# Reading a two-byte scalar by a 16-partition broadcast instead of a single-partition load, in a streaming multiply-add

## The chip, the cores and the metric

One core of a Trainium2 chip. The metric is device time in microseconds (us) of one execution; the median of several executions is quoted. The kernel before takes 152.79 us (3 runs, 152.72 to 152.88). The profile's own span, from the first to the last instruction, is about 1.8 us shorter (150.6 us).

## The reference

```python
B, S, D = 512, 32, 640            # x, fx: bf16; alpha: one bf16 number
def reference(x, fx, alpha):
    return x + alpha * fx
```

x, fx and the result are 20.97 MB each: 62.9 MB have to be moved for one multiply and one add per element.

## The kernel before

The tensors are seen as 128 partitions of 81,920 elements and cut into five chunks of 16,384 columns (4 MB each, 32 KB per partition). All bulk transfers go through SyncE's queue; alpha alone goes through ScalarE's. TensorE multiplies a row of ones by alpha, which puts alpha on all 128 partitions, and VectorE copies it out of PSUM.

```python
def alpha_to_lanes(nc, consts, psum, alpha, eng):     # eng = nc.scalar
    P = nc.NUM_PARTITIONS
    a_1 = consts.tile([1, 1], alpha.dtype, name="a_1")
    eng.dma_start(out=a_1[:], in_=alpha[None, :])
    ones = consts.tile([1, P], alpha.dtype, name="ones")
    nc.vector.memset(ones[:], 1.0)
    a_ps = psum.tile([P, 1], F32, name="a_ps")
    nc.tensor.matmul(a_ps[:], ones[:], a_1[:], start=True, stop=True)
    a_f = consts.tile([P, 1], F32, name="a_f")
    nc.vector.tensor_copy(out=a_f[:], in_=a_ps[:])
    return a_f

# ... cut: views, pools (four buffers for x, two for fx), load_x, load_f, store ...
    a_f = alpha_to_lanes(nc, consts, psum, alpha, nc.scalar)

    def compute(k, parts=1):                # x_t = f_t * a_f + x_t, on VectorE
        n = CHUNK // parts
        for j in range(parts):
            s = bass.ts(j, n)
            nc.vector.scalar_tensor_tensor(
                out=xt[k][:, s], in0=ft[k][:, s], scalar=a_f[:],
                in1=xt[k][:, s], op0=ALU.mult, op1=ALU.add)

    load_x(0); load_f(0); load_x(1); load_f(1); load_x(2)
    compute(0)                              # first reader of a_f
    load_f(2); store(0); load_x(3)
    compute(1)
    # ... cut: the same pattern to chunk 4, whose store is cut in two
```

## Time and profile before

| what | value | where it is read |
|---|---|---|
| time | 152.79 us | the timed runs |
| DMA engines | 418 GB/s, 9 tenths busy or more nearly throughout | the slices of the page |
| VectorE | 86.9 us busy, 49.5 us waiting for fx | the page, the view of waits |
| alpha landed | 1.87 us | the trace's semaphore records |
| first multiply-add starts | 22.84 us | the timeline |

First the page of the kernel before: its span, the busy tenths of the DMA engines and the GB/s in 40 slices of 3.8 us, and the packets. q1 is SyncE's queue, q10 is ScalarE's.

```profile
span 150.6 us, 85 instructions
DMA  6999999999999999799999999999999999999994
GB/s 200 444 453 435 418 418 418 418 444 453 444 453 435 418 418 418 339 444 470 418 418 418 418 418 435 435 435 453 426 435 444 418 418 435 435 435 405 426 444 205
DMA packets 2306, 62.92 MB, mean 418 GB/s; under 512 B 258, under 2 KB 258, under 8 KB 258
q10 hardware_dynamic: 2, 0.00, 0.0%
```

There is no slice in which the DMA engines rest: the kernel is a stream of transfers. The packets can be counted: 2048 rows of data and 256 semaphore packets (the 4-byte write with which an engine reports its share of a transfer as moved; 16 bulk transfers of 16 each) on q1, and on q10 one 2-byte data packet and one 4-byte semaphore packet, alpha's.

The start of the timeline of the kernel before. Columns: start in us, duration in us, engine (ACTq and SPq are the issuing queues), line, operation, and in brackets how long the engine had been idle and what released it.

```profile
0.73 0.38 SPq L59 DMA_DIRECT2D x_t<-in_x_dram  x1
0.73 0.49 ACTq L20 DMA_DIRECT2D a<-in_alpha_dram  x1
1.92 0.16 PE L24 MATMUL a_ps<-a,ones 1*128 1x1 bf16 x1 [1.92 <-DMA a<-in_alpha_dram]
2.11 0.16 DVE L26 COPY a_f<-a_ps 128x1 f32<-128x1 f32 x1 [1.13 <-PE a_ps L24]
22.84 17.28 DVE L69 SCALAR_TENSOR_TENSOR x_t<-f_t,a_f,x_t 128x16384 bf16<-128x16384 bf16 x1 [20.57 <-DMA f_t<-in_fx_dram]
```

a_f is ready at 2.27 us, and its first reader starts at 22.84 us, released by the load of f_t. Alpha has 20.6 us of slack to its first use.

The view of waits of the kernel before (engine, line, what it waited for: us in all, times, longest):

```profile
DVE x_t L69 <- DMA f_t<-in_fx_dram: 49.5, 5, 20.6
PE a_ps L24 <- DMA a<-in_alpha_dram: 1.9, 1, 1.9
```

Two lines of its chain of waits (start, duration, what):

```profile
40.16 21.99 DMA f_t<-in_fx_dram
79.55 41.16 DMA f_t<-in_fx_dram
```

### The profile page before, as it was taken

Reading aid. Unit: us, or ns where it says so; the run is one execution under the profiler, and the core shown is the slowest. Engines: PE = TensorE matmul, PEld = TensorE weight load, DVE = VectorE, ACT = ScalarE, POOL = GpSimd, SP = SyncE. Lnnn points to the kernel's source line nnn. Section 1 sums busy time; section 2 is a strip of 40 time slices with the busy share of each in tenths; the row PEclk is TensorE's granted clock in tenths of the full one; section 3 lists DMA queues with packets and bytes.
Section 4 is the critical chain, followed back from the end, with each engine's and each line's share of the span. In section 5 each row is a group of like instructions: output and inputs, shape, how many; then the busy total and the mean of one; then the engine's idle time right before and its main releaser. Section 6 shows DMA issues by size and latency. Waiting matters only on the chain.

```text
span 150.6 us, 85 instructions
## 1 busy us (share of the span) xinstructions
PE 0.2 (0%) x1; PEld 0.1 (0%) x1; DVE 86.9 (58%) x8; POOL 0.2 (0%) x4
## 2 busy tenths in 40 slices
PE   0000000000000000000000000000000000000000
PEld 0000000000000000000000000000000000000000
DVE  0000009999679998499991006999900089997000
POOL 0000000000000000000000000000000000000000
DMA  6999999999999999799999999999999999999994
GB/s 200 444 453 435 418 418 418 418 444 453 444 453 435 418 418 418 339 444 470 418 418 418 418 418 435 435 435 453 426 435 444 418 418 435 435 435 405 426 444 205
DMA packets 2306, 62.92 MB, mean 418 GB/s; under 512 B 258, under 2 KB 258, under 8 KB 258
## 3 DMA queue, kind: packets, MB, share of 16 engines
q1 hardware_dynamic: 2304, 62.92, 98.0%
q10 hardware_dynamic: 2, 0.00, 0.0%
HBM read 41.94 MB, written 20.97 MB: 418 GB/s over the span
## 4 chain that ended last, share of the span: by engine, by line
DMA 56%; DVE 29%; DVEq 6%; issue 0%; SPq 0%
DMA f_t<-in_fx_dram 56%; DVE x_t L69 29%; DVEq L131 6%; SPq L59 0%; DVEq L69 0%
## 5 line engine op out<-in xcount | busy, mean ns | idle before, releaser
L69 DVE SCALAR_TENSOR_TENSOR x_t<-f_t,a_f,x_t 128x16384 bf16<-128x16384 bf16 (+1 forms) x6 | 86.6, 14439 | 49.5 <-DMA f_t<-in_fx_dram 49.5
L26 DVE COPY a_f<-a_ps 128x1 f32<-128x1 f32 x1 | 0.2, 159 | 1.1 <-PE a_ps L24 1.1
L22 DVE MEMSET ones<- 1x128 bf16 x1 | 0.2, 165 | 0.8 <-PEq L120 0.8
L24 PE MATMUL a_ps<-a,ones 1*128 1x1 bf16 x1 | 0.2, 159 | 1.9 <-DMA a<-in_alpha_dram 1.9
L120 POOL MEMSET const-bfloat16-1.0<- 128x1 bf16 x1 | 0.1, 102 | 0.0
L120 POOL MEMSET const-uint8-127<- 128x1 uint8 x1 | 0.1, 102 | 0.0
L24 PEld LDWEIGHTS <-ones 1*128 1x128 bf16 x1 | 0.1, 100 | 1.0 <-DVE ones L22 1.0
L120 POOL MEMSET const-float32-0.0<- 128x1 f32 x1 | 0.1, 99 | 0.2 <-issue 0.2
L120 POOL MEMSET const-float32-1.0<- 128x1 f32 x1 | 0.1, 99 | 0.0
## 6 DMA issues: line engine op xcount, KB each, us to landing
x_t<-in_x_dram SPq DMA_DIRECT2D x5, 4096.0 KB, 34.8
f_t<-in_fx_dram SPq DMA_DIRECT2D x5, 4096.0 KB, 32.1
out_dram<-x_t SPq DMA_DIRECT2D x4, 4096.0 KB, 36.5
out_dram<-x_t SPq DMA_DIRECT2D x2, 2048.0 KB, 15.2
a<-in_alpha_dram ACTq DMA_DIRECT2D x1, 0.0 KB
```

Source lines behind the costliest of these rows:

```text
L22: nc.vector.memset(ones[:], 1.0)
L24: nc.tensor.matmul(a_ps[:], ones[:], a_1[:], start=True, stop=True)
L26: nc.vector.tensor_copy(out=a_f[:], in_=a_ps[:])
L69: nc.vector.scalar_tensor_tensor(out=xt[k][:, s], in0=ft[k][:, s], scalar=a_f[:], in1=xt[k][:, s], op0=ALU.mult, op1=ALU.add,)
L120: nc = _bacc.Bacc("TRN2", target_bir_lowering=False, num_devices=1)
L131: with _tile.TileContext(nc) as tc:
```

## The change

Alpha is loaded to 16 partitions by one broadcast transfer, so that each of the 16 DMA engines makes one 2-byte read; the matmul still takes only the first row. The likely intent is to spread the little transfer over the engines rather than to leave it on one.

```diff
-    a_1 = consts.tile([1, 1], alpha.dtype, name="a_1")
-    eng.dma_start(out=a_1[:], in_=alpha[None, :])
+    a_1 = consts.tile([16, 1], alpha.dtype, name="a_1")
+    eng.dma_start(out=a_1[:], in_=alpha.to_broadcast((16, 1)))
     ones = consts.tile([1, P], alpha.dtype, name="ones")
     nc.vector.memset(ones[:], 1.0)
     a_ps = psum.tile([P, 1], F32, name="a_ps")
-    nc.tensor.matmul(a_ps[:], ones[:], a_1[:], start=True, stop=True)
+    nc.tensor.matmul(a_ps[:], ones[:], a_1[0:1, :], start=True, stop=True)
```

## The prediction

> **What bounds the kernel now.** The DMA engines. The slices row of the page shows them at 9 tenths nearly throughout, 418 GB/s over the span of 150.6 us. The trace's packet records add up: 1792 rows of 32 KB at 1.213 us (median) and 256 of 16 KB at 0.611 us make 112 x 1.213 + 16 x 0.611 = 145.6 us on each of 16 engines. The first bulk packet starts at 1.74 us and the last store lands at 149.76 us, 148.0 us in all, so only about 2.4 us of an engine's stretch is not steady streaming. VectorE is busy 86.9 us (58%) and waits 49.5 us for the fx loads (the view of waits). The chain of waits is 56% DMA of f_t.
>
> **Where alpha stands.** The timeline: its transfer is issued at 0.73 us on ScalarE's queue (0.49 us of issue), the matmul starts at 1.92 us, the copy to a_f is over at 2.27 us. The first multiply-add waits for f_t until 22.84 us. Alpha's chain has 20.6 us of slack. It now moves two packets (2 bytes of data, 7 ns; 4 bytes of semaphore, 9 ns), at 1.58 us, just ahead of the first bulk packet.
>
> **What the change does.** It adds 15 data and 15 semaphore packets, one pair on each engine: an estimate from the two records is 16 ns of busy time an engine. The Trainium skill ("DMA: Bandwidth & Descriptors", section "Why a DMA increments its semaphore by 16 and not by 1") says that a [1,1] scalar uses one engine and that the slowest dimension of both sides sets the number, so 16 here. This trace agrees for before: one data packet, and two updates of alpha's semaphore (1.30 us, 1.87 us). Bytes moved, the order of the bulk transfers, the matmul (1x1), the copy and VectorE's work stay as they are.
>
> **Worth.** (a) Alpha's chain: if its packets queue behind the first bulk packets (1.6 to 2.4 us long), it lands at about 3.5 to 4.5 us instead of 1.87 us; still 18 us of slack, so nothing. (b) Busy time: 0.02 us an engine. (c) What can reach the end is a later start of the bulk stream, since the stream is the bound: 16 engines' descriptors of alpha are made at the same time as those of the first x load. The issues in the timeline take 0.33 to 0.57 us; a delay of 0 to 0.3 us of the first load is my estimate from those. (d) Evening out one 16 ns pair over the engines gains nothing.
>
> **Prediction.** 152.9 us, 8 times in 10 within 152.3 to 153.6 us. Faster by over 2%: 1%; within 2%: 98%; slower by over 2%: 1%.
>
> **What shows each step.** Alpha's queue: 32 packets instead of 2; packets under 512 B 288 instead of 258. Idle time of TensorE before the matmul: 1.9 us now, between 1.9 and 4.5 us after. Start of the first multiply-add: 22.8 us, later by no more than 0.3 us, ended by DMA f_t and not by a_f. Gap between 418 GB/s and after's mean: under 0.3%. VectorE busy time: 86.9 us unchanged. First bulk packet: 1.7 to 2.0 us.
>
> **What would make it wrong.** Alpha landing after 22 us, because its packets starve behind the bulk queue on some engine (then the first multiply-add would name the matmul's copy); a lasting phase shift between engines that slows the loads and stores together; or the tiny reads of one address stalling an engine for several us rather than for 16 ns.

## The result, and the profile after

The changed kernel takes 152.84 us (4 runs, 152.58 to 152.95), the kernel before on the same occasions 152.75 us (4 runs, 152.33 to 152.88). The ratio is 1.0008 with a 95% interval of 0.9985 to 1.0031: the same. (A ratio here is the mean time of one kernel's fast runs over the mean of the other's fast runs of the same rounds, so it is not quite the ratio of the medians quoted.)

The page of the changed kernel:

```profile
span 151.0 us, 85 instructions
DMA  6999999999999999899999999999999999998994
GB/s 208 443 434 434 425 417 417 434 443 451 443 434 434 417 417 399 347 460 434 425 434 417 417 417 425 451 469 434 417 443 417 417 425 425 460 469 360 425 443 187
DMA packets 2336, 62.92 MB, mean 417 GB/s; under 512 B 288, under 2 KB 288, under 8 KB 288
q10 hardware_dynamic: 32, 0.00, 0.0%
```

30 more tiny packets, as expected, and the same stream. Now the start of its timeline:

```profile
0.73 0.57 ACTq L20 DMA_DIRECT2D a<-in_alpha_dram  x1
0.73 0.38 SPq L59 DMA_DIRECT2D x_t<-in_x_dram  x1
8.19 0.16 PE L24 MATMUL a_ps<-a,ones 1*128 1x1 bf16 x1 [8.19 <-DMA a<-in_alpha_dram]
8.38 0.16 DVE L26 COPY a_f<-a_ps 128x1 f32<-128x1 f32 x1 [7.41 <-PE a_ps L24]
22.84 17.29 DVE L69 SCALAR_TENSOR_TENSOR x_t<-f_t,a_f,x_t 128x16384 bf16<-128x16384 bf16 x1 [14.30 <-DMA f_t<-in_fx_dram]
```

The matmul starts at 8.19 us instead of 1.92 us. Alpha comes 6.3 us later than before, and the first multiply-add starts at 22.84 us, as before. The view of waits of the changed kernel says the same, and shows how a wait off the critical path grows without a price:

```profile
DVE x_t L69 <- DMA f_t<-in_fx_dram: 43.5, 5, 14.3
PE a_ps L24 <- DMA a<-in_alpha_dram: 8.2, 1, 8.2
```

VectorE's wait for f_t has even shrunk by 6 us, from 49.5 to 43.5 us. That is no gain: the idle time before the first multiply-add is counted from the copy of alpha, which now comes 6.3 us later. Only the end of that idle time matters.

The profiled span is 0.4 us longer than before (151.0 against 150.6 us). The chain of waits of the changed kernel says where the two part:

```profile
40.16 22.44 DMA f_t<-in_fx_dram
80.00 41.03 DMA f_t<-in_fx_dram
```

Up to 40.16 us the two chains agree to within 0.01 us. The difference arises between 40 and 63 us, over 30 us after alpha's last packet. The kernel before, a second time (below), has there

```profile
40.16 22.27 DMA f_t<-in_fx_dram
```

and a span of 151.0 us itself. The 0.4 us are how one execution differs from another, not the change.

So the time is explained quickly. What was unexpected is the 8.19 us. The packet records of the trace carry no engine number, but packets of one engine follow each other without a gap, so they can be joined end to start. One engine of the changed kernel (start us; b a 32 KB bulk packet, A2 alpha's data, A4 alpha's semaphore packet), and the engine that carried alpha before:

```
after : b 1.75  b 3.42  b 4.67  A2 5.88  b 5.88  A4 7.09  b 7.10  b 8.31
before: A2 1.58  A4 1.59  b 1.74  b 3.57  b 4.80
```

Before, alpha's pair reached its engine 0.15 us ahead of the bulk stream and was through in 16 ns. After, the joined records show three bulk packets ahead of the data packet on all the engines that could be joined without doubt, and one more between the data and the semaphore packet. The 16 data packets start at 5.88 to 6.62 us, the 16 semaphore updates come at 7.47 to 8.15 us.

The Trainium skill ("DMA: Bandwidth & Descriptors", section "Why a DMA increments its semaphore by 16 and not by 1") says that on these queues only the engines used post an update and the sequencer writes the remainder at once. Both traces agree: before, two updates of alpha's semaphore (1.30 us from the sequencer, 1.87 us from the one engine); after, 16.

### The profile page after: what moved, and what is told of

It is laid out like the page before. It is cut to its first block, busy times and chain, and to the rows that moved or that the text cites. A ratio compares the mean times of both kernels' runs of the same rounds, so it can differ in the third digit from the quotient of the medians.

```text
span 151.0 us, 85 instructions
## 1 busy us (share of the span) xinstructions
PE 0.2 (0%) x1; PEld 0.1 (0%) x1; DVE 86.9 (58%) x8; POOL 0.2 (0%) x4
## 4 chain that ended last, share of the span: by engine, by line
DMA 56%; DVE 29%; DVEq 6%; issue 0%; SPq 0%
DMA f_t<-in_fx_dram 56%; DVE x_t L69 29%; DVEq L131 6%; SPq L59 0%; DVEq L69 0%
## 5 line engine op out<-in xcount | busy, mean ns | idle before, releaser
L69 DVE SCALAR_TENSOR_TENSOR x_t<-f_t,a_f,x_t 128x16384 bf16<-128x16384 bf16 (+1 forms) x6 | 86.5, 14438 | 43.5 <-DMA f_t<-in_fx_dram 43.5
```

Source lines behind the costliest of these rows:

```text
L69: nc.vector.scalar_tensor_tensor(out=xt[k][:, s], in0=ft[k][:, s], scalar=a_f[:], in1=xt[k][:, s], op0=ALU.mult, op1=ALU.add,)
```

## The experiments

Theory A: alpha's transfer has to wait its turn behind bulk packets on every engine; all of that falls into the slack before the first multiply-add, so it costs nothing. Rivals: R, the extra 0.4 us of span is a real cost; B, a 16-row broadcast is slow in itself, or its packets come at a fixed time. Every result was numerically correct, all profiles that could be judged were of the fast state.

### 1. The same two kernels again: after_again, before_again

No edit. Five rounds each on one chip; the second is the kernel before as if it were a change.

> The changed kernel once more, with more rounds. If the change costs nothing on the critical path (theory A: all of it falls into the slack before the first multiply-add): ratio to before between 0.998 and 1.002, alpha lands near 8 us with three bulk packets ahead of it on every engine, first multiply-add near 22.8 us. If the 0.4 us that the profiled span gained is a real cost of the change (rival R): ratio 1.002 to 1.004 with an interval that leaves out 1.

> The kernel before, submitted as if it were a change: the noise of the comparison. Both theories: ratio 1.000, within 0.997 to 1.003. It is the yardstick for the ratio of the changed kernel: if this one strays as far as that, that ratio says nothing.

Measured: changed kernel 152.87 us (6 runs), ratio 0.9985 (0.9962 to 1.0008); kernel before as a change 152.77 us (6 runs), ratio 0.9981 (0.9957 to 1.0005), both against the same 11 runs of before (median 153.17 us, 152.68 to 154.24). Alpha lands at 8.16 us, as in the other profile. The first multiply-add of the changed kernel starts at 23.02 us here (22.84 us in the other profile), that of before at 22.84 us. The changed kernel strays no further from before than before strays from itself; the mean of its six runs over that of the six is 152.88 / 152.81 = 1.0004. R falls: there is no cost that these runs can see, and a gain of the change is not there either.

### 2. The broadcast ahead of the bulk loads: alpha_first_sp

```diff
-    a_f = alpha_to_lanes(nc, consts, psum, alpha, nc.scalar)
+    a_f = alpha_to_lanes(nc, consts, psum, alpha, nc.sync)
```

> The same 16-row transfer, but issued on SyncE's queue ahead of all bulk loads. Theory A (alpha was late because three bulk packets stood before it on every engine): alpha lands near 2 us, as in the kernel before, although it uses 16 engines. Rival B (a 16-row broadcast is slow by itself): it lands near 8 us here too. Its issue (0.4 to 0.6 us) delays the first bulk load: since the stream is the bound, first multiply-add at 23.2 to 23.4 us instead of 22.84, and the time rises by 0.3 to 0.6 us (ratio 1.002 to 1.004).

Measured: 153.57 us, ratio 1.0032 (1.0009 to 1.0056), which is 0.5 us; against the six runs of before_again it is 0.8 us (mean 153.60 against 152.81). From its timeline:

```profile
0.73 0.57 SPq L20 DMA_DIRECT2D a<-in_alpha_dram  x1
1.36 0.55 SPq L59 DMA_DIRECT2D x_t<-in_x_dram  x1
2.56 0.16 PE L24 MATMUL a_ps<-a,ones 1*128 1x1 bf16 x1 [2.56 <-DMA a<-in_alpha_dram]
23.56 17.28 DVE L69 SCALAR_TENSOR_TENSOR x_t<-f_t,a_f,x_t 128x16384 bf16<-128x16384 bf16 x1 [20.64 <-DMA f_t<-in_fx_dram]
```

The 16-row transfer lands at 2.5 us when nothing stands before it: 16 rows are not slow, rival B's first form falls. It also shows what does cost: the first bulk load is issued 0.63 us later and its issue takes 0.55 instead of 0.38 us, the first bulk packet starts at 2.54 instead of 1.74 us, the first multiply-add starts 0.72 us later, and the time rises by 0.5 to 0.8 us, depending on which runs of before it is held against. The ratio is inside the expected 1.002 to 1.004; the first multiply-add, expected at 23.2 to 23.4 us, is later than that, because the slower issue of the first load was not in the sum. In this kernel, which is one stream, a late start is paid in full or nearly so.

The packet records of this run show one thing more. With nothing before them, the 16 data packets start at 2.06 to 2.24 us, 1.3 us after the issue. The single packet of the kernel before, issued at the same 0.73 us (on ScalarE's queue), started at 1.58 us, and the first bulk packet of the changed kernel at 1.75 us. So the 16-row transfer is not slow, but it is about half a microsecond later off the mark (an estimate from these two runs), enough to lose the race with a bulk load that is issued at the same moment. That this is how alpha fell behind in the changed kernel fits the times, but was not tried apart.

### 3. One engine, but late: one_engine_late

From the kernel before: the row that alpha is written to is first cleared by VectorE, which holds the transfer back.

```diff
-    a_1 = consts.tile([1, 1], alpha.dtype, name="a_1")
-    eng.dma_start(out=a_1[:], in_=alpha[None, :])
+    a_1 = consts.tile([1, 4096], alpha.dtype, name="a_1")
+    nc.vector.memset(a_1[:], 0.0)
+    eng.dma_start(out=a_1[:, 0:1], in_=alpha[None, :])
...
-    nc.tensor.matmul(a_ps[:], ones[:], a_1[:], start=True, stop=True)
+    nc.tensor.matmul(a_ps[:], ones[:], a_1[:, 0:1], start=True, stop=True)
```

> The kernel before, with alpha on one engine, but its transfer held back some 2 to 4 us by a memset of the row that it writes to, so it is issued when the bulk stream runs. Theory A: being on 16 engines is not the point, standing behind the bulk packets is: the single data packet starts 2.5 to 5 us after the issue, its semaphore packet one bulk packet (1.2 us) after that, landing 4 to 6.5 us after the issue. Rival B (16 rows are slow, one row is fast): landing about 1.2 us after the issue, as in the kernel before (0.73 to 1.87 us).

Measured (one look, 152.83 us): from its timeline

```profile
3.01 0.49 ACTq L21 DMA_DIRECT2D a<-in_alpha_dram  x1
8.96 0.16 PE L25 MATMUL a_ps<-a,ones 1*128 1x1 bf16 x1 [8.96 <-DMA a<-in_alpha_dram]
```

Its single data packet starts at 7.35 us, 4.3 us after the issue, its semaphore packet at 8.57 us, one bulk packet later, and it lands 5.9 us after the issue. As theory A has it. A transfer on one engine waits about as long as one on 16 when it comes after the stream has begun. Being ahead of the stream made alpha quick in the kernel before; being on one engine may have mattered in that it got alpha there first (1.58 us, experiment 2).

### 4. Smaller bulk packets ahead: x0_quarters, x0_halves, x0_eighths

The changed kernel, with the first x load cut into n loads along the columns (n = 4; then 2 and 8), so that its packets are 8, 16 or 4 KB instead of 32 KB.

```diff
-        nc.sync.dma_start(out=xt[k][:], in_=xv[:, bass.ts(k, CHUNK)])
+        parts = 4 if k == 0 else 1            # 2, 8 in the other two
+        n = CHUNK // parts
+        for j in range(parts):
+            nc.sync.dma_start(
+                out=xt[k][:, bass.ts(j, n)],
+                in_=xv[:, k * CHUNK + j * n : k * CHUNK + (j + 1) * n])
```

> The changed kernel with the first x load cut into four loads of 4096 columns, so its packets are 8 KB (0.30 us estimated as a quarter of 1.21) instead of 32 KB. Theory A (alpha's packets wait for a fixed number of bulk packets on each engine: three before the data, one before the semaphore): the wait shrinks with the packets; the first data packet starts at 2.5 to 3.5 us and alpha lands at 3 to 4.5 us. Rival B (its descriptors are made late, or 16 rows are slow, at a fixed time): first data packet still near 5.9 us, landing near 8 us.

Measured: not as either side had it. The data packets start at 4.84 to 5.27 us, after the whole first quarter (8 packets and its semaphore packet) on nearly every engine, not after three packets. So three rules were set against each other in the next two runs.

> The changed kernel with the first x load cut into two loads of 8192 columns: 16 KB packets of 0.61 us. Where do alpha's data packets start on the engines? Rule T (behind the whole first transfer, or three packets, whichever is shorter): behind three packets, at 3.9 to 4.4 us. Rule W (behind about 64 to 96 KB of bulk): behind 4 to 6, at 4.4 to 6 us. Rule F (they come to the engines at a fixed time of about 4.6 to 4.8 us and take the next turn): at 4.6 to 5.4 us, whatever the packets.

> The changed kernel with the first x load cut into eight loads of 2048 columns: 4 KB packets, 0.15 us by a quarter of the 16 KB and 8 KB ones. Rule T: behind the first transfer (8 packets and its semaphore), at 3.0 to 3.8 us. Rule W: behind 16 to 24 packets, at 4.3 to 5.8 us. Rule F: at 4.6 to 5.0 us.

The line of the view of waits that tells when alpha had landed, for the eighths, the quarters and the halves in turn:

```profile
PE a_ps L24 <- DMA a<-in_alpha_dram: 4.7, 1, 4.7
```

```profile
PE a_ps L24 <- DMA a<-in_alpha_dram: 5.8, 1, 5.8
```

```profile
PE a_ps L24 <- DMA a<-in_alpha_dram: 6.8, 1, 6.8
```

| bulk packets ahead | alpha's data packets start, us | usual number ahead | matmul starts, us |
|---|---|---|---|
| 4 KB (eighths) | 3.42 to 4.16 | 8 and a semaphore | 4.75 |
| 8 KB (quarters) | 4.84 to 5.27 | 8 and a semaphore | 5.78 |
| 16 KB (halves) | 5.30 to 5.73 | 5 | 6.76 |
| 32 KB (changed kernel) | 5.88 to 6.62 | 3 | 8.19 |

In the runs with 4 and 8 KB packets the semaphore packet leaves its engine within 0.01 us of the data packet; with 16 and 32 KB packets one bulk packet stands between the two.

None of the three rules holds in both runs: T misses the halves (expected 3.9 to 4.4 us), W misses the eighths (expected 4.3 to 5.8 us), F misses both, narrowly in the halves. What they do show is that the wait shrinks steadily with the packets of the bulk load that stands ahead, so no fixed time explains it; the second form of rival B falls. (Cutting the load also makes two to eight issues out of one; the two were not separated.) What decides whether three, five or eight packets are ahead stays open.

The Trainium skill ("DMA: Bandwidth & Descriptors", section "Queues, rings and completion order") says that an engine goes round its queues packet by packet and gives 9 to 17 descriptors as a typical packet. The turn taking is what the traces show. The size is not what they show at 32 KB: there a turn, once alpha's queue was being served, was a single 32 KB record (bulk 5.88, semaphore 7.09, bulk 7.10 us), if a record of the trace is one descriptor. The whole first transfer of nine records ahead, as with 4 and 8 KB, would fit the page's number.

The times, 152.57, 152.21 and 152.14 us, are single looks beside runs of before that lie between 152.22 and 153.75 us in those two sets: no version here can be called faster.

### 5. How much slack there is: alpha_after_x1, alpha_after_f1

The call of `alpha_to_lanes` moved to SyncE's queue, behind `load_x(1)` in the first and behind `load_f(1)` in the second kernel.

```diff
-    a_f = alpha_to_lanes(nc, consts, psum, alpha, nc.scalar)
...
     load_x(1)
+    a_f = alpha_to_lanes(nc, consts, psum, alpha, nc.sync)   # alpha_after_x1
     load_f(1)                        # in alpha_after_f1 the call stands below this
```

> The 16-row transfer issued on SyncE's queue behind x0, f0 and x1: in that queue's order it lands near 32 us, so the first multiply-add starts at 32.2 to 32.6 us, 9.5 us late, and ends near 49.7 us, while the loads already issued keep the engines busy until 51.9 us. Theory A' (what counts is whether the DMA engines run dry, not when the multiply-add starts): ratio 0.997 to 1.005. Rival (delay of the first multiply-add passes on to the end): about 162 us, ratio 1.06.

> The same, one load further back, behind f1: landing near 42 us, first multiply-add 42.2 to 59.5 us, while the loads that were issued end at 51.9 us. So the DMA engines stand idle for 7 to 8 us: time 159 to 163 us (ratio 1.04 to 1.07) by theory A'. It is the control that shows the slack does end. If the time stays within 1%, the slack is larger than I believe; if it rises by 19 us, the delay passes on whole.

Measured: 155.25 us, ratio 1.0139 (1.0093 to 1.0184), and 163.85 us, ratio 1.0730 (1.0706 to 1.0753). The first multiply-adds start at 33.02 and 42.74 us: 10.2 and 19.9 us late. The time rises by about 2 to 2.5 us and by 11 us.

In alpha_after_f1 the stream stands still. From its timeline (the two multiply-adds that follow each other are merged):

```profile
42.74 34.48 DVE L68 SCALAR_TENSOR_TENSOR x_t<-f_t,a_f,x_t 128x16384 bf16<-128x16384 bf16 x2
60.05 0.33 SPq L62 DMA_DIRECT2D f_t<-in_fx_dram  x1
```

The view by windows (window, its length, busy us of four engines with the number of instructions, clock, DMA share, GB/s; packets seem to be counted where they start, so a share can pass 1):

```profile
51.00:52.00 1.00, 0.00 (x0) 0.00 (x0) 1.00 (x1) 0.00 (x0) 1.00 0.00 0
52.00:60.00 8.00, 0.00 (x0) 0.00 (x0) 8.00 (x2) 0.00 (x0) 1.00 0.00 0
60.00:61.00 1.00, 0.00 (x0) 0.00 (x0) 1.00 (x2) 0.00 (x0) 1.00 0.00 0
61.00:62.00 1.00, 0.00 (x0) 0.00 (x0) 1.00 (x1) 0.00 (x0) 1.00 1.97 524
```

The loads already issued have landed at 51.8 us, the multiply-add that frees the next buffer ends at 60.0 us, and the first packet after that starts at 61.0 us. I had expected 7 to 8 us of idle and 159 to 163 us; it was 9 us, because 1 us passes from issue to first packet, and the first packets after a standstill last up to 2.4 us instead of 1.21 us, as they do at the start of the kernel.

alpha_after_x1 went as neither side expected (unchanged, or 162 us). Its profile is of the slowest of its four executions, 156.15 us. Its timeline and the same view:

```profile
33.02 51.68 DVE L68 SCALAR_TENSOR_TENSOR x_t<-f_t,a_f,x_t 128x16384 bf16<-128x16384 bf16 x3
50.34 0.33 SPq L62 DMA_DIRECT2D f_t<-in_fx_dram  x1
```

```profile
50.00:51.00 1.00, 0.00 (x0) 0.00 (x0) 1.00 (x2) 0.00 (x0) 1.00 0.46 197
51.00:52.00 1.00, 0.00 (x0) 0.00 (x0) 1.00 (x1) 0.00 (x0) 1.00 1.56 426
52.00:53.00 1.00, 0.00 (x0) 0.00 (x0) 1.00 (x1) 0.00 (x0) 1.00 0.26 98
```

The next load is issued at 50.34 us and its first packet starts at 51.28 us, while the engines had their last packets at 50.8 to 51.4 us (landed at 51.2 to 51.8 us). The margin was expected to be 2.2 us (49.7 to 51.9 us); it came out as 1.5 us (50.3 to 51.8 us), and the start-up of that load used it up: its first packets start at 51.28 us on the first engine and at 52.5 us on the last. Summed over the packet records, 0.46 us an engine is idle at 50 to 60 us, bulk packets take 1.2 to 1.3 us an engine more in all than before, and at the end the engines finish up to 3.2 us apart (last store's landings 150.31 to 153.51 us) instead of 0.8 us (148.96 to 149.76 us). Why they drift apart is not settled.

So the real limit for alpha is not its first use at 22.84 us but the point where the stream would run dry. At 33 us it is already past; where between 23 and 33 us it lies was not tried. The changed kernel's 8.2 us is far inside.

### 6. More tiny packets: bcast128, dose_all, dose_one

bcast128 loads alpha to all 128 partitions and drops the ones, the matmul and PSUM; the copy reads `a_1`.

```diff
+    a_1 = consts.tile([P, 1], alpha.dtype, name="a_1")
+    eng.dma_start(out=a_1[:], in_=alpha.to_broadcast((P, 1)))
...                                          # ones, a_ps and matmul removed
-    nc.vector.tensor_copy(out=a_f[:], in_=a_ps[:])
+    nc.vector.tensor_copy(out=a_f[:], in_=a_1[:])
```

> Alpha broadcast to all 128 partitions, so eight data packets an engine, with no matmul. Theory A with strict alternation of the two queues, one packet each: data near 6 us, then one alpha packet per bulk packet of 1.21 us: 7 more for the data and 1 for the semaphore, landing at 15 to 17 us. If the engine takes all eight in one turn: landing near 8 us. In both cases before 22.8 us, so ratio 0.998 to 1.003. Slow only if the packets starve past 22.8 us.

Measured: 153.71 us, ratio 1.0037 (1.0013 to 1.0060), which is 0.6 us; it is 0.9 us above before_again on the same chip (means 153.68 and 152.81). From its timeline and its slices:

```profile
15.88 0.15 DVE L22 CAST a_f<-a 128x1 f32<-128x1 bf16 x1 [15.88 <-DMA a<-in_alpha_dram]
24.49 17.28 DVE L65 SCALAR_TENSOR_TENSOR x_t<-f_t,a_f,x_t 128x16384 bf16<-128x16384 bf16 x1 [8.46 <-DMA f_t<-in_fx_dram]
GB/s 233 362 371 371 448 414 423 423 423 457 448 431 431 423 414 431 448 457 423 440 423 414 423 414 457 440 448 431 414 414 431 423 466 448 440 414 392 423 436 138
```

One alpha packet to one bulk packet is what the records show nearly throughout, and alpha lands at 15.85 us, inside the expected 15 to 17 us. The place in that range is partly luck: the first data packets start at 4.68 to 5.24 us, behind two bulk packets and not three, so three is no fixed number even for 32 KB; and the bulk packets beside them are slower (1.32 us on average from 3.3 to 16 us) than the sum had them. And there is a cost that was not expected: slices 2 to 4 run at 362 to 371 GB/s, where the changed kernel has 434 to 443, and the first multiply-add starts 1.65 us late though alpha was there long before. That raised the question whether a tiny packet costs an engine far more than its 9 ns record. dose_all and dose_one put useless copies of alpha behind the real one, in the kernel before:

```diff
     a_f = alpha_to_lanes(nc, consts, psum, alpha, nc.scalar)
+    junk = consts.tile([P, 4], alpha.dtype, name="junk")             # dose_all
+    for j in range(4):
+        nc.scalar.dma_start(out=junk[:, j : j + 1], in_=alpha.to_broadcast((P, 1)))
```

```diff
     a_f = alpha_to_lanes(nc, consts, psum, alpha, nc.scalar)
+    junk = consts.tile([1, 18], alpha.dtype, name="junk")            # dose_one
+    for j in range(18):
+        nc.scalar.dma_start(out=junk[:, j : j + 1], in_=alpha[None, :])
```

> The kernel before, plus four useless broadcasts of alpha to 128 partitions: 32 data and 4 semaphore packets more on every engine (the changed kernel has one of each). Theory S (a tiny packet between bulk packets costs its engine far more than its record of 9 ns: in the 128-row run the first multiply-add came 1.65 us late for 9 packets an engine, 0.18 us each): 36 packets cost 3 to 6.5 us of the stream, time 155.5 to 159 us. Rival Z (the records are the cost, 9 ns each): 0.3 us, under 153.5 us. In the trace: alternation one to one until about 50 us, bulk packets beside them at 1.3 to 1.4 us instead of 1.213.

> The kernel before, plus 18 useless transfers of alpha to one partition: 18 data and 18 semaphore packets, all on one engine. If a tiny packet costs its engine 0.18 us and a bulk transfer waits for its slowest engine: that engine falls behind by 3 to 6.5 us, the spread of landings of one load grows from 0.6 us to 3 us and more, time 154 to 159 us. If only many tiny packets at once (or many readers of one address) are slow: spread and time stay as before, within 0.5%.

dose_all: 153.52 us, ratio 1.0074 (1.0034 to 1.0114); about 1.1 us for 36 packets an engine, where 9 packets had cost 0.6 to 0.9 us. Neither theory holds. From its timeline and its slices:

```profile
24.26 17.29 DVE L72 SCALAR_TENSOR_TENSOR x_t<-f_t,a_f,x_t 128x16384 bf16<-128x16384 bf16 x1 [21.96 <-DMA f_t<-in_fx_dram]
GB/s 216 424 355 381 424 415 415 415 424 459 424 433 467 424 415 415 415 433 450 415 467 441 424 415 415 415 459 433 441 459 424 415 415 415 450 424 411 441 428 199
```

Only the first of the four broadcasts costs anything. It runs beside the first x load, up to 17 us (144 tiny packets from 4 to 17 us): slices 3 and 4 are at 355 and 381 GB/s, bulk packets that start between 8.9 and 16 us average 1.338 us instead of 1.213 us, and the first multiply-add starts at 24.26 us, 1.42 us late. The other three (432 tiny packets from 17 to 47 us) run beside bulk packets of 1.213 us on average (17 to 40 us), the same as in before. So in these runs a tiny packet between two bulk packets is as good as free once the stream is steady. Why many of them are dear in the first 16 us stays open.

dose_one: 157.27 us, ratio 1.0312 (1.0274 to 1.0350), inside the range that I had given for a slow engine, and yet for another reason. Its view of waits of SyncE's queue, a line of its timeline, and its slices:

```profile
SPq L66 <- DMA junk<-in_alpha_dram: 13.7, 1, 13.7
14.79 0.33 SPq L66 DMA_DIRECT2D f_t<-in_fx_dram  x1
GB/s 227 446 404 0 404 404 413 463 455 421 404 421 480 438 413 404 354 446 413 404 455 455 438 404 413 463 438 430 413 430 463 413 421 421 438 446 383 451 421 160
```

The load of f_t was issued only at 14.79 us, after one of the junk transfers had landed, and the DMA engines stood still for a whole slice. This is a wait in the program: the trace shows eight completion semaphores for all transfers, used again in turn, and the first load of fx has the one of a junk transfer and waits for it. On the engine that carried the junk, bulk packets follow each other every 1.21 to 1.24 us while it has tiny packets in between (4.64 to 11.95 us: six packets, 1.22 us each). The slow engine that I had expected is not there; the experiment was confounded by its own semaphores. In dose_all the same sharing delayed the issue of the third x load to 13.76 us, but transfers were queued before it, so nothing ran dry.

## Why the prediction was right

- **The bound.** Right. The stream of bulk transfers decides: a start 0.72 us later cost 0.5 to 0.8 us (alpha_first_sp), an alpha 6.3 us later cost nothing.
- **The packet counts.** Right: 32 packets on alpha's queue, 288 packets under 512 B.
- **The bulk stream's start.** Right: first bulk packet at 1.75 us (1.74 us before), first multiply-add at 22.84 us (23.02 us in after_again), mean 417 GB/s, VectorE 86.9 us. The delay of 0 to 0.3 us that made the forecast 152.9 us did not show; this term was 0.01 us. That the measured 152.84 us lies within 0.1 us of the forecast is therefore luck: executions of both kernels lie between 152.33 and 152.95 us. What was right is that the time would not move.
- **"it lands at about 3.5 to 4.5 us instead of 1.87 us".** The mechanism, waiting behind bulk packets, was right; the size was wrong. I counted one bulk packet ahead. There were three before the data packet (from 1.75 to 5.88 us on the engine shown) and a fourth before the semaphore packet (to 7.09 us), so it landed at 8.15 us and TensorE waited 8.2 us, outside the 1.9 to 4.5 us that the prediction names. With 18 us of slack assumed and 14.7 us left, this did not reach the time.
- **"Busy time: 0.02 us an engine".** Not contradicted for the change itself: bulk packets between 3.3 and 16 us average 1.221 us in the changed kernel and 1.215 us in before. In the second profiles they are 1.235 and 1.216 us; but there the changed kernel's packets are slower from 17 to 40 us too (1.225 against 1.213 us), long after alpha, so this is not shown to come from the tiny packets. A cost of 0.1 to 0.2 us lies below what the timed runs can tell. As a general rule it was incomplete: eight data packets an engine in the first 16 us delayed the first multiply-add by 1.65 us.
- **The slack as 20 us.** It is the distance to the first use. The distance that matters, to the point where the stream runs dry, was not in the prediction; an alpha at 32.6 us costs 1.4%, one at 42.4 us costs 7.3%.

## What to carry to other kernels

In a kernel that is one unbroken stream of transfers, ask of a small change only whether it delays the start of the stream or makes it run dry; waits of other engines may grow fourfold (1.9 to 8.2 us here) at no cost. A small transfer that must be early has to be issued so that it reaches the engines before the bulk transfers, and here one packet on one engine was there sooner (1.58 us) than 16 on 16 engines (2.06 us). Once the stream ran, alpha waited behind two to eight bulk packets for its data and, with packets of 16 and 32 KB, behind one more for its semaphore, on one engine as on sixteen. And when you add transfers as an experiment, look for new waits on shared semaphores before you read the time: dose_one landed in the expected range by another cause.

## What the Trainium skill lacked or had wrong

- "DMA: Bandwidth & Descriptors", section "Queues, rings and completion order": it gives the turn of a queue as 9 to 17 descriptors, typically. Beside 32 KB rows the turn was a single row of 1.21 us once both queues were served, and a newcomer found 3 rows of 32 KB (2 in bcast128), 5 of 16 KB, or a whole transfer of 8 rows of 8 or 4 KB ahead of it. The section does not say what decides this; these runs do not either.
- The same page gives no latency for a small transfer that joins a running stream: 5.9 us from issue to landing on one engine (issued at 3.01 us) and 7.4 us on sixteen (issued with the first load), against 1.1 us for one that came first.
- The same page has nothing on what many 2-byte packets do to a stream of large ones beside them: 9 an engine in the first 16 us cost 0.6 to 0.9 us of time, 27 an engine from 17 to 47 us cost nothing that could be seen.
- The same page, section "Latency and other measured facts", gives about 0.6 us to the first byte on these queues. For bulk loads the runs agree if it is counted from the end of the issue (1.11 to 1.74 us in the kernel before, 60.38 to 61.00 us in alpha_after_f1); alpha, with nothing ahead of it, took 0.36 us on one engine (1.22 to 1.58 us in the kernel before) and 0.76 us on 16 (1.30 to 2.06 us in alpha_first_sp). The section lacks what follows: the first packet of each engine lasted 1.2 to 2.4 us instead of 1.21 us, at the start as after a standstill.
